# One core, attention into a mixture of experts: when a planner puts eight small transfers on the SP queue

## The chip, the core and the metric

The kernel runs as one program on one core of a Trainium2 chip. Its time is device microseconds of one execution: 771.33 us is the median of three (770.04 to 773.77). The engines work side by side, each through its own list of instructions: PE (matmul), DVE and ACT (elementwise), POOL, and SP, which computes nothing here and issues DMA transfers from one queue; an instruction whose wait isn't over holds those behind it in its list.

## The reference, cut to what matters

Three layers follow one another on 3072 tokens of width 384:

```python
x = attn(q, k, v, alpha)                      # a decaying state per head, scanned over 768 steps
expert_idx = argmax(logits(x), 1)             # 8 experts; gate_w = the winner's softmax share
out[mask] = gate_w[mask, None] * (relu(x[mask] @ w1[e]) @ w2[e])   # per expert e, 384 -> 1024 -> 384
h = out @ w_in                                # 384 -> 2048, float64 weights
return maximum(0.01 * h, h) @ w_out           # 2048 -> 384
```

Every product of weights is done as three float16 products of a high and a low half (hi*hi, hi*lo, lo*hi) that are summed in PSUM.

## The kernel before, in words

**Three stages.** The first (to about 168 us) does the attention and the routing, and scatters each token's row into a DRAM buffer `bucket`, sorted by expert; a row holds the 384 values, a scale, the gate and the token's number. The second (168 to 400 us) runs the experts 0 to 7 one after the other. The third (400 us to the end) is the dense layer, with results scattered by token.

**An expert.** It takes up to 432 rows of `bucket` (`CAP`). `gather` loads them (`xg`), `block` scales and splits them on ACT (L977) and DVE (L978) into four pieces `xs`, and transposes each piece with a DMA from SP's queue (L980) into `xt`. `up` multiplies `xt` by `w1` (L1038 to L1040, eight groups of nine matmuls) and splits the relu on ACT and DVE (L1045, L1046); `down` multiplies by `w2` (L1064 to L1066, three groups of 24) and writes the result into the columns of `x2` that belong to the expert (L1075 on ACT is the high half, L1076 on DVE the low half; the planner calls the latter `("x2l", e, d)`). `xt`, the weight sets and the PSUM tiles are double or fourfold, so the next expert's inputs are made while one runs.

**Weights.** They come as float32 through five staging tiles `wstage` (`fetch`, L989, 384 KB each), and ACT and DVE split them: L994 and L995 for expert weights (eight pieces an expert), L1011 to L1017 for the third stage's float64 weights (`double`, four pieces an expert). A fetch must wait until the staging tile of five fetches earlier has been read.

**Scales and tokens.** `put_meta(e)` (L938 to L944) copies two numbers of each of the expert's 432 rows from `bucket` to a compact DRAM buffer `meta`, at an offset that SP loads from SBUF (L941, for e above 0). The transfers of successive experts overlap in `meta`, so each waits until the one before has landed. `scales` (L948) loads `meta` into `ms` after the last, and a cast on DVE (L949) makes the token numbers `tki`. Both are first used in the third stage.

**Clears.** `clear` zeroes the columns of `x2` above the first expert's, 12 ACT instructions (L1085), before expert 1 writes there.

**The planner.** The order of the second stage's instructions on each engine is computed ahead by `Plan`: a list schedule in which an operation has an engine, a duration, the keys it reads and writes, and `at`. It takes the operation that can start first; `at` decides only among those within 0.15 us of it. An operation that depends on another of the same engine may start when that one has been *issued*, without its landing:

```python
t = max([free.get(eng, 0.0)] + [end[d] + self.HOP if ops[d][0] != eng else start[d] + ops[d][1] for d in deps])
...
first = min(best)[0]
t, _, _, i = min((b for b in best if b[0] <= first + 0.15), key=lambda b: b[1:])
```

The keys named in `after` are dependencies of the plan alone. The waits that the engines obey come from the tiles and buffers that an instruction reads and writes. `begin(e)` is 5.5 + 26.4 e.

Of the kernel before, what the change touches and what calls it, by code (L numbers as in the profile page):

```python
# [34 lines left out]
CAP = 432  # L35
# [140 lines left out]
def body(ctx, tc, qT, kT, aT, v, emb, tau, w1, w2, w_in, w_out, out):  # L176
# [6 lines left out]
    bucket = dram.tile([E * NT, AUG], F32, name="bucket")  # L183
    bviews = dram_disjoint_views(bucket, NC)
    meta = dram.tile([X2, 2], F32, name="meta")
# [62 lines left out]
    class Jobs:  # L248
# [20 lines left out]
        def add(self, jobs):  # L269
            self.todo += jobs  # L270
            self.fetch()
# [11 lines left out]
    with tc.tile_pool(name="at", bufs=1) as rt, \  # L283
# [58 lines left out]
        plan = Plan()  # L342
        NU = B * NP
        V, S_, T_, G_, Q_ = "DVE", "ACT", "PE", "POOL", "SP"
# [556 lines left out]
    with tc.tile_pool(name="mx", bufs=1) as mxp, \  # L901
# [10 lines left out]
        size = [min(P, CAP - n * P) for n in range(NB)]  # L912
        NF = CAP // P
        plan = Plan(rate=230e3, land=4.0)
        V, S_, T_, G_, Q_ = "DVE", "ACT", "PE", "POOL", "SP"
        START, TURN = 5.5, 26.4

        def begin(e):
            return START + TURN * e

        def gather(e):
            xg = xgs[e % 2]

            def block(n):
                nc.sync.dma_start(xg[:size[n], n], bucket[e * NT + n * P:e * NT + n * P + size[n]])

            def most():
                nc.sync.dma_start(xg[:, :NF], bucket[e * NT:e * NT + NF * P].rearrange("(n p) d -> p n d", p=P))
                for n in range(NF, NB):
                    block(n)  # L930

            if e < 2:
                for n in range(0 if e else E0 // P, NB):
                    plan.add(Q_, 0.45, lambda n=n: block(n), ["bucket"], [("xg", e), ("row", e, n)], size=(P * AUG * 4, 2.5), at=float(e))
            else:
                plan.add(Q_, 0.9, most, ["bucket"], [("xg", e % 2)] + [("row", e % 2, n) for n in range(NB)], size=CAP * AUG * 4, at=begin(e - 2) + 8,
                         after=[("xt", 1, NB - 1, 0)] if e == 2 else ())

        def put_meta(e):
            def go():  # L940
                so = nc.sync.value_load(offi[0:1, e:e + 1], min_val=0, max_val=NT) if e else 0  # L941
                nc.sync.dma_start(meta[ds(so, CAP) if e else slice(0, CAP)], bucket[e * NT:e * NT + CAP, D + 1:D + 3])

            plan.add(Q_, 1.5, go, ["bucket"], ["meta"], at=begin(e) + 4, size=(CAP * 64, 5.0))  # L944

        def scales():

# [21 lines left out]
        def block(e, n):  # L969

            m, g = size[n], len(turned) % 4
            turned.append(n)
            x, r = xgs[e % 2][:m, n, :D], xgs[e % 2][:m, n, D:D + 1]
            xs, xt = xs16[g][:m], xts[e % 2]
            at = begin(e - 1) + 1.0 + 4.0 * n if e > 1 else n - 15.0
            got = ("row", e % 2, n)
            plan.add(S_, 0.62, lambda: nc.scalar.activation(xs[:, 0], x, AF.Copy, scale=r), [got], [("xs", g, 0)], at=at)  # L977
            plan.add(V, 0.61, lambda: nc.vector.scalar_tensor_tensor(xs[:, 1], x, r, xs[:, 0], op0=ALU.mult, op1=ALU.subtract),  # L978
                     [got, ("xs", g, 0)], [("xs", g, 1)], at=at)
            plan.add(Q_, 1.25, lambda: nc.sync.dma_start_transpose(out=xt[:, :, n * P:n * P + m], in_=xs.rearrange("p i d -> p (i d)")),  # L980
                     [("xs", g, i) for i in range(2)], [("xt", e % 2, n, i) for i in range(2)], size=(230e3, 5.0), at=at + 1.0)
# [50 lines left out]
        def up(e, f, xt, at, cols, early=False):  # L1032
            (w1h, w1l), n = shaped(sets[e % 2])[:2], cols.stop - cols.start
            ps, hh, hl = ps1[f % 4][:, :n], hid[0][f][:, cols], hid[1][f][:, cols]

            def go():
                for k in range(KD):
                    nc.tensor.matmul(ps, w1h[:, f, k], xt[:, k], start=k == 0, stop=False)  # L1038
                    nc.tensor.matmul(ps, w1h[:, f, k], xt[:, KD + k], start=False, stop=False)  # L1039
                    nc.tensor.matmul(ps, w1l[:, f, k], xt[:, k], start=False, stop=k == KD - 1)  # L1040

            rows = [("sg", i) for i in range(2)] if early else [("xt", e % 2, b, i) for b in range(cols.start // P, NB) for i in range(2)]
            key = ("h", f, early)
            plan.add(T_, 9 * step(n), go, [("w", e % 2, 0, f // 2, i) for i in range(2)] + rows, [("ps1", f % 4)], at=at)
            plan.add(S_, 0.16 + n / 1200, lambda: nc.scalar.activation(hh, ps, AF.Relu), [("ps1", f % 4)], [(*key, 0)], at=at)  # L1045
            plan.add(V, 0.155 + n / 960, lambda: nc.vector.scalar_tensor_tensor(hl, ps, 0.0, hh, op0=ALU.max, op1=ALU.subtract), [("ps1", f % 4), (*key, 0)], [(*key, 1)], at=at)  # L1046
# [3 lines left out]
        def places(e):  # L1050
            def on(eng, n):
                offset[n] = eng.value_load(offi[0:1, e:e + 1], min_val=0, max_val=NT)

            plan.add(S_, 0.1, lambda: on(nc.scalar, 0), [], [("place", 0)], at=begin(e) + 4)
            plan.add(V, 0.1, lambda: on(nc.vector, 1), [], [("place", 1)], at=begin(e) + 4)

        def down(e, d, at, cols, early=False):
            (w2h, w2l), n = shaped(sets[e % 2])[2:], cols.stop - cols.start
            b = (KD * e + d) % 4
            ps, ds_ = ps2[b][:, :n], slice(d * P, (d + 1) * P)  # L1060

            def go(f):
                hh, hl = hid[0][f][:, cols], hid[1][f][:, cols]
                nc.tensor.matmul(ps, w2h[:, f, ds_], hh, start=f == 0, stop=False)  # L1064
                nc.tensor.matmul(ps, w2h[:, f, ds_], hl, start=False, stop=False)  # L1065
                nc.tensor.matmul(ps, w2l[:, f, ds_], hh, start=False, stop=f == NF1 - 1)  # L1066

            for f in range(NF1):
                plan.add(T_, 3 * step(n), lambda f=f: go(f), [("w", e % 2, 1, f // 2, i) for i in range(2)] + [("h", f, early, i) for i in range(2)], [("ps2", b)], at=at + 0.05 * f)

            def place(i):
                return cols if e == 0 else ds(offset[i], CAP)

            where = [[("place", i)] * (e > 0) + [("clear", i, d)] * (e == 1) for i in range(2)]
            plan.add(S_, 0.16 + n / 1200, lambda: nc.scalar.activation(x2[0][d][:, place(0)], ps, AF.Copy, scale=2.0 ** -8), [("ps2", b)] + where[0], [("x2", e, d)], at=at)  # L1075
            plan.add(V, 0.155 + n / 960, lambda: nc.vector.scalar_tensor_tensor(x2[1][d][:, place(1)], ps, 2.0 ** -8, x2[0][d][:, place(1)], op0=ALU.mult, op1=ALU.subtract),  # L1076
                     [("ps2", b), ("x2", e, d)] + where[1], [("x2l", e, d)], at=at)

        def clear(d, at):

            w = (NT - CAP) // 4
            for n in range(2):
                for o in range(CAP, NT, 2 * w):
                    x = x2[n][d][:, o:o + 2 * w].bitcast(F32)
                    plan.add(S_, 0.16 + w / 1200, lambda x=x: nc.scalar.activation(x, row0[:, 0:1].to_broadcast([P, w]), AF.Copy), ["bucket"], [("clear", n, d)], at=at)  # L1085
# [5 lines left out]
        def pieces_of(e):  # L1091
            mine = [(begin(e) + 4.0 + 2.9 * j, weights, e + 1, j) for j in range(2 * KD * F1 // CH if e + 1 < E else 0)]
            mine += [(begin(e) + 5.0 + 5.8 * j, *second[e * per + j]) for j in range(min(per, len(second) - e * per))]
            return sorted(mine, key=lambda x: x[0])
# [16 lines left out]
        for e in range(E):  # L1111
            if e:
                add(pieces_of(e))
            cols = slice(0 if e else E0, CAP)
            for f in range(NF1):
                up(e, f, xts[e % 2][:, :, cols], begin(e) + 1.65 * f - 12.0, cols)
                if e + 1 < E and f < NB:
                    block(e + 1, f)
                if f == 2:
                    put_meta(e)  # L1120
                if f == 4 and e + 2 < E:
                    gather(e + 2)
            if e:
                places(e)
            for d in range(KD):
                down(e, d, begin(e) + 13.2 + 4.4 * d - 12.0, cols)
            if e == 0:
                for d in range(KD):
                    clear(d, begin(1) + 4.0 * d)
        scales()  # L1130
        for i in plan.order():
            plan.ops[i][2]()
# [2 lines left out]
    with tc.tile_pool(name="gp", bufs=1) as gp:  # L1135
# [9 lines left out]
        plan = Plan()  # L1145
# [240 lines left out]
```

## Time and profile before

| | us |
|---|---|
| median of three executions | 771.33 |
| the profiled execution, its own time | 768.53 |
| its span, first to last instruction | 766.8 |
| PE busy | 730.8 (95%) |
| DVE busy | 602.4 (79%) |
| ACT busy | 389.0 (51%) |
| the chain that ended last: PE | 81% of the span |
| the same: DMA `meta<-bucket` | 3% of the span |

A group of the profile names the source line, the engine, the operation and its tiles as out<-in. In the timelines, the first two numbers are start and duration in us, and square brackets hold the idle time ahead of the instruction and what ended it. In the span cut into 40 slices of 19.2 us, PE is at 9 tenths or more in the second and third stages except in slices 8 and 11 to 12 counted from 0, and the slice 230 to 249 us has PE at 4 tenths and its granted clock at 6 tenths.

### The profile page before, as it was taken

How to read it: one execution, taken by the hardware profiler on the slowest of the kernel's cores; microseconds unless marked ns; L12 is line 12 of the kernel's file. 1: busy time of each engine (PE TensorE's matmuls, PEld its weight loads, DVE VectorE, ACT ScalarE, POOL GpSimd, SP SyncE). 2: the span in 40 equal slices, each digit the busy share in tenths (PEclk: the TensorE clock that was granted, in tenths of full speed). 3: DMA queues.
4: the chain of work that ended last, by engine and by line, in shares of the span. 5: the costliest groups of instructions: out<-in, count | busy, mean ns of one | idle time of the engine just before them, and what ended most of it. 6: DMA issues, size and time to landing. Idle time of an engine off the chain costs nothing.

```text
span 766.8 us, 16571 instructions
## 1 busy us (share of the span) xinstructions
PE 730.8 (95%) x6775; PEld 561.6 (73%) x6775; DVE 602.4 (79%) x1131; ACT 389.0 (51%) x746; POOL 87.6 (11%) x91
## 2 busy tenths in 40 slices
PE   7999999989984999999999999999999999999995
PEld 3777766658742555555558777999999999999995
DVE  7989889967727887889879888878778768778771
ACT  2343455537916666777656444544434435535430
POOL 4120715150000000000000010010110110110101
PEclk9999999999996999999999999999999999999999
DMA  8983946247829866878610000000000000000001
GB/s 295 340 272 130 276 151 208 64 146 191 195 34 286 239 201 192 246 212 209 194 60 1 12 12 11 12 23 1 22 22 1 23 22 2 22 12 12 21 11 35
DMA packets 61968, 84.70 MB, mean 110 GB/s; under 512 B 29880, under 2 KB 41152, under 8 KB 61888
## 3 DMA queue, kind: packets, MB, share of 16 engines
q1 hardware_dynamic: 58656, 74.09, 33.8%
q0 software_dynamic: 3072, 9.49, 3.3%
q8 instruction: 55, 0.90, 0.5%
q14 instruction: 25, 0.20, 0.1%
q10 hardware_dynamic: 160, 0.01, 0.0%
HBM read 66.83 MB, written 12.12 MB: 103 GB/s over the span
## 4 chain that ended last, share of the span: by engine, by line
PE 81%; DMA 7%; DVE 7%; ACT 3%; issue 1%; POOL 0%; SPq 0%; POOLq 0%; DVEq 0%; ACTq 0%
PE ps L829 8%; PE ps L828 8%; PE ps L827 8%; PE ps L861 6%; PE ps L863 6%; PE ps L862 6%; PE ps L1038 4%; PE ps L1039 4%; PE ps L1040 4%; PE ps L1066 4%; PE ps L1065 4%; PE ps L1064 4%; DMA meta<-bucket 3%; PE psc L409 2%; PE py L462 2%; DMA wstage<-in_w 2%
## 5 line engine op out<-in xcount | busy, mean ns | idle before, releaser
L827 PE MATMUL ps<-x2h,wih 128*128 128x256 f16 x576 | 157.0, 273 | 0.0
L828 PE MATMUL ps<-x2l,wih 128*128 128x256 f16 x576 | 157.0, 273 | 0.0
L829 PE MATMUL ps<-x2h,wil 128*128 128x256 f16 x576 | 157.0, 273 | 0.0
L835 DVE TENSOR_TENSOR held<-ps,held 128x512 f32<-128x512 f32 x96 | 65.8, 686 | 51.3 <-ACT held L834 51.3
L834 ACT ACTIVATE held<-ps 128x512 f32<-128x512 f32 x96 | 57.2, 596 | 78.1 <-PE ps L829 77.9
L895 POOL DMA_INDIRECT out<-wstage,tki x24 | 25.4, 1060 | 559.2 <-ACT wstage L1202 302.3
L1038 PE MATMUL ps<-xt,w1h 128*128 128x432 f16 (+1 forms) x192 | 64.3, 336 | 15.7 <-DMA xt<-xs 14.8
L1065 PE MATMUL ps<-held,w2h 128*128 128x432 f16 (+2 forms) x216 | 70.2, 326 | 0.5 <-DVE held L1046 0.5
L1066 PE MATMUL ps<-held,w2l 128*128 128x432 f16 (+2 forms) x216 | 70.2, 326 | 0.0
L1064 PE MATMUL ps<-held,w2h 128*128 128x432 f16 (+2 forms) x216 | 70.2, 326 | 0.0
L1039 PE MATMUL ps<-xt,w1h 128*128 128x432 f16 (+1 forms) x192 | 64.3, 336 | 0.5 <-DVE xt L964 0.5
L1040 PE MATMUL ps<-xt,w1l 128*128 128x432 f16 (+1 forms) x192 | 64.3, 336 | 0.0
L827 PEld LDWEIGHTS <-wih 128*128 128x128 f16 x576 | 56.4, 98 | 6.8
L828 PEld LDWEIGHTS <-wih 128*128 128x128 f16 x576 | 56.4, 98 | 6.7
L829 PEld LDWEIGHTS <-wil 128*128 128x128 f16 x576 | 56.4, 98 | 6.5
L1045 ACT ACTIVATE held<-ps 128x432 f16<-128x432 f32 (+2 forms) x72 | 35.2, 489 | 26.6 <-PE ps L1040 22.6
L1046 DVE SCALAR_TENSOR_TENSOR held<-ps,held 128x432 f16<-128x432 f32 (+2 forms) x72 | 39.3, 552 | 11.8 <-ACT held L1045 11.6
L1038 PEld LDWEIGHTS <-w1h 128*128 128x128 f16 x216 | 21.6, 100 | 32.4 <-issue 15.8
L874 DVE SCALAR_TENSOR_TENSOR wstage<-ps,ms,wstage 128x192 f32<-128x192 f32 x80 | 31.9, 411 | 16.6 <-PE ps L863 16.5
L349 PE MATMUL pfill<-busy,ones 128*128 128x512 f16 x122 | 40.0, 400 | 2.0 <-POOL busy L194 2.0
L846 ACT ACTIVATE o1h<-held 128x256 f16<-128x256 f32 (+1 forms) x40 | 20.9, 523 | 30.7 <-DVE held L835 29.9
L846 ACT ACTIVATE o0h<-held 128x256 f16<-128x256 f32 (+1 forms) x40 | 20.9, 523 | 30.3 <-DVE held L835 29.7
(267 smaller groups left out, 1904.8 us busy)
## 6 DMA issues: line engine op xcount, KB each, us to landing
wstage<-in_w SPq DMA_DIRECT2D x64, 384.0 KB, 4.2
a<-in_aT SPq DMA_DIRECT2D x16, 387.5 KB, 5.4
k<-in_kT SPq DMA_DIRECT2D x16, 384.0 KB, 5.9
q<-in_qT SPq DMA_DIRECT2D x16, 384.0 KB, 6.6
wstage<-in_w_in SPq DMA_DIRECT2D x16, 384.0 KB, 4.4
wstage<-in_w_out SPq DMA_DIRECT2D x16, 384.0 KB, 3.4
v<-in_v SPq DMA_DIRECT2D x8, 576.0 KB, 8.8
xg<-bucket SPq DMA_DIRECT2D x6, 582.0 KB, 5.7
```

The lines of the kernel that those rows point to most:

```text
L827: nc.tensor.matmul(d, wih[:, k, fs], xs[0][k], start=k == 0, stop=False)
L828: nc.tensor.matmul(d, wih[:, k, fs], xs[1][k], start=False, stop=False)
L829: nc.tensor.matmul(d, wil[:, k, fs], xs[0][k], start=False, stop=k == KD - 1)
L834: add("ACT", 0.59, lambda: nc.scalar.activation(dst, src, AF.Copy, scale=0.01), [key], [("g", i)])
L835: add("DVE", 0.69, lambda: nc.vector.tensor_tensor(dst, src, dst, op=ALU.max), [key, ("g", i)], [("g", i)])
L861: nc.tensor.matmul(d, oh, wh, start=k == 0, stop=False)
L1038: nc.tensor.matmul(ps, w1h[:, f, k], xt[:, k], start=k == 0, stop=False)
L1039: nc.tensor.matmul(ps, w1h[:, f, k], xt[:, KD + k], start=False, stop=False)
L1040: nc.tensor.matmul(ps, w1l[:, f, k], xt[:, k], start=False, stop=k == KD - 1)
L1064: nc.tensor.matmul(ps, w2h[:, f, ds_], hh, start=f == 0, stop=False)
L1065: nc.tensor.matmul(ps, w2h[:, f, ds_], hl, start=False, stop=False)
L1066: nc.tensor.matmul(ps, w2l[:, f, ds_], hh, start=False, stop=f == NF1 - 1)
```

## The change

Two arguments to the planner. `put_meta(e)` for e above 0 gets an `after` on `("x2l", e - 1, 0)`, the low half of the first third of the preceding expert's result, and is entered with 0.9 us instead of 1.5. The clears get an earlier `at`. What the instructions do stays; only their order on the engines can differ.

```diff
-            plan.add(Q_, 1.5, go, ["bucket"], ["meta"], at=begin(e) + 4, size=(CAP * 64, 5.0))
+            plan.add(Q_, 0.9, go, ["bucket"], ["meta"], at=begin(e) + 4, size=(CAP * 64, 5.0), after=[("x2l", e - 1, 0)] if e else ())
...
-                    clear(d, begin(1) + 4.0 * d)
+                    clear(d, begin(0) + 8.0 + 4.0 * d)
```

## Rows read from the trace of the kernel before

**Rows 1.** Timeline of PE: start, duration, instruction, in brackets idle and releaser.

```profile
199.95 0.35 PE L1038 MATMUL ps<-xt,w1h 128*128 128x432 f16 x1
...
226.05 0.35 PE L1066 MATMUL ps<-held,w2l 128*128 128x432 f16 x1
241.18 0.52 PE L1038 MATMUL ps<-xt,w1h 128*128 128x432 f16 x1 [14.78 <-DMA xt<-xs]
...
244.37 0.43 PE L1038 MATMUL ps<-xt,w1h 128*128 128x432 f16 x1
...
387.35 0.35 PE L1064 MATMUL ps<-held,w2h 128*128 128x432 f16 x1
```

**Rows 2.** Busy time of stretches: length; PE, PEld, DVE, ACT, POOL; PE clock, DMA share, GB/s.

```profile
190.00:200.00 10.00, 9.50 (x126) 9.35 (x124) 8.69 (x20) 10.00 (x23) 0.00 (x0) 1.00 0.83 207
...
219.00:222.50 3.50, 3.50 (x21) 1.89 (x20) 0.00 (x0) 0.00 (x0) 0.00 (x0) 1.00 0.07 1
...
241.20:244.40 3.20, 3.20 (x10) 1.32 (x11) 2.87 (x7) 2.13 (x5) 0.00 (x0) 0.50 1.11 341
...
295.70:321.90 26.20, 26.20 (x146) 14.06 (x144) 23.86 (x42) 20.42 (x39) 0.00 (x0) 1.00 0.79 221
```

**Rows 3.** Chain that ended last, 197 to 246 us: start, duration, what.

```profile
200.22 6.36 DMA meta<-bucket
...
221.91 3.82 DMA meta<-bucket
...
225.74 0.40 SPq L948
...
226.25 4.97 DMA wstage<-in_w
...
234.17 6.92 DMA xt<-xs
```

**Rows 4.** Timeline of SP's queue in the second stage, merged where a line repeats.

```profile
188.18 7.18 SPq L980 DMA_TRANSPOSE xt<-xs  x4
...
211.19 11.26 SPq L942 DMA_DIRECT2D meta<-bucket  x4
...
227.95 2.62 SPq L980 DMA_TRANSPOSE xt<-xs  x2
...
372.31 1.23 SPq L989 DMA_DIRECT2D wstage<-in_w  x2
```

**Rows 5.** Timeline of DVE in the second stage.

```profile
203.32 0.56 DVE L1013 SCALAR_TENSOR_TENSOR t<-wstage,t 128x384 uint32<-128x384 uint32 x1
...
215.89 0.60 DVE L978 SCALAR_TENSOR_TENSOR xs<-xg,xs 48x384 f16<-48x384 f32 x1
232.53 0.56 DVE L1017 SCALAR_TENSOR_TENSOR wil<-t,wih 128x384 f16<-128x384 f32 x1 [16.03 <-ACT wih L1016]
...
367.86 0.61 DVE L1076 SCALAR_TENSOR_TENSOR x2l<-ps,x2h 128x432 f32 x1 [1.40 <-ACT x2h L1075]
...
385.96 0.95 DVE L995 SCALAR_TENSOR_TENSOR w2l<-wstage,w2h 128x768 f16<-128x768 f32 x1
```

**Rows 6.** All instructions of a tile, durations min/median/max in ns; then landing in us.

```profile
L980 SPq DMA_TRANSPOSE xt<-xs x28: 1187/1223/2904, 188.2 to 345.9; - x28
...
DMA to landing us min/median/max: 2.5/4.2/6.9
```

**Rows 7.** Timeline of ACT: the first and the last of the 12 clears, and a later weight.

```profile
181.95 0.74 ACT L1085 ACTIVATE x2h<-row 128x660 f32<-128x660 f32 x1
...
205.98 0.74 ACT L1085 ACTIVATE x2l<-row 128x660 f32<-128x660 f32 x1
...
378.29 0.84 ACT L994 ACTIVATE w2h<-wstage 128x768 f16<-128x768 f32 x1
```

**Rows 8.** First use of `ms`, by source line: durations in ns, first and last start.

```profile
L1202 ACT ACTIVATE wstage<-ps,ms x4: 580/580/581, 436.0 to 481.0; 128x384 f32<-128x384 f32 x4
```

## The prediction

> **What bounds the kernel now.** I read the page's 40 slices first: the one place after the attention where PE falls far below full is the slice 230 to 249 us, and its clock falls there too. The timeline of PE shows why: the last matmul of expert 1 starts at 226.05, the first of expert 2 at 241.18, held by the DMA that transposes its tokens [rows 1]. Everywhere else from 244 us to the end of the expert stage PE is full: the turn of expert 4, 26.2 us long, has 26.20 busy at clock 1.00 [rows 2]. The chain of waits then tells what made the transposes late. From 200.22 it goes through six `meta<-bucket` landings one after the other to the `ms` load at 225.74, a weight fetch at 226.25, and the transpose at 234.17 that lands at 241.09 [rows 3]. SP's queue issues four of these metas in a row from 211.19, and nothing else between [rows 4]. Each of these transfers of 864 numbers stops the queue for 3.8 to 6.4 us [rows 3], because the next must wait for its landing. In 219.0 to 222.5 neither DVE nor ACT does anything, and the DMA engines are at 0.07 [rows 2]: the feed is starved, not slow.
>
> The cause is readable in the planner. It lets an SP operation start when the SP operation it depends on was issued, so the chain of metas looks to it like 1.5 us fillers for any idle moment of SP. It had idle moments, and put all eight ahead of expert 2: the `ms` load, which follows the last, was issued at 225.74 [rows 3].
>
> **What the change removes.** The six `meta` landings and the `ms` load leave the stretch 200 to 226. With `after` on a DVE result, each meta can be planned only once the preceding expert's first third is out, so metas 1 to 7 come about one turn apart, and each finds its predecessor long landed: no wait on SP. PE then passes from expert 1 to 2 as early as the inputs allow.
> - Cadence: 199.95 to 226.05 is 143 steps, 0.1825 us each, so expert 1 would hand over at 226.23 [rows 1]. The gap is 241.18 - 226.23 = 14.95 us.
> - Clock: nine matmuls from 241.18 to 244.37 take 3.19 us where nine steps are 1.64 [rows 1]; the clock was granted at 0.50 (1.2 GHz) in that stretch, after the idle, and at 1.00 in a turn without idle [rows 2]. That is 1.55 us more, which goes with the idle time.
> - Together 16.5 us, the ceiling of this part.
>
> **What is late next.** Expert 2's first group needs all four transposed pieces. Their last DVE half was done at 215.89 + 0.60 = 216.5 [rows 5]. A staging tile for the weight fetch that went out at 226.25 was free after 203.32 + 0.56 = 203.9 [rows 5], so that fetch and the transposes queued behind it [rows 4] can go some 20 us earlier. From 216.5, a transpose lands 2.5 to 6.9 us later, median 4.2 [rows 6], so at 219.0 to 223.4: before 226.23. But with SP unblocked, more weight pieces reach DVE earlier and may be ordered ahead of that last half: two at 0.95 us [rows 5] and their companions on ACT at 0.84 [rows 7], up to 4 us. That gives 219 to 227.4, an idle time of 0 to 1.2 us; with a second delay of the same size for a full DMA system (the share was 1.11 in 241.2 to 244.4 [rows 2]) 0 to 5. By the median it is 216.5 + 1.9 + 4.2 = 222.6, so I take 0 and keep 5 as the end.
>
> DVE lost 16.03 us to the same stall [rows 5], so the feed moves forward by about as much as PE does and their distance later on stays. This matters, as a turn has 23.86 us of DVE work in 26.2 [rows 2]: there is no room to catch up much.
>
> **What the moved metas cost.** Issue time is the same as before. On the DMA engines one meta alone took 0.07 of 3.5 us [rows 2], 0.25 us of all sixteen; seven beside the weights are 1.7 us in seven turns that leave about a fifth of the DMA time free (0.79 in use [rows 2]). Nothing, then; at worst a whole landing of 6.4 us [rows 3] is added once to a fetch behind it.
>
> The last one is different. `ms` must still wait for meta 7 to land, and it now does so near the end of expert 6, just after an x2l like that at 367.86 [rows 5], with `w2` of expert 7 behind it on SP. The planner still ignores that wait. SP would be held for 3.8 to 6.4 us [rows 3]; of the fetches behind it, those issued from 372.31 wait 0 to 3 us, and the first of these is converted at 378.29 [rows 7], some 6 us after its issue, where a fetch took 4.97 to land [rows 3]. The cast of the token numbers can hold DVE some 3 us for the same reason. The last piece of `w2` for expert 7 is ready at 386.91 [rows 5]; PE needs it near 390.6: the down part starts at 387.35 [rows 1], and 18 steps of 0.1825 precede the quarter that reads it. So 3.7 us of cover: cost 0 to 3, I take 0. The use of `ms` at 436.0 [rows 8] stays some 60 us away.
>
> The Trainium skill prices such a wait lower: in "DMA: Bandwidth & Descriptors", section "Anatomy of one DMA", the fixed part of a transfer is put at about 2.0 us, fitted on transfers that GpSimd issues. By that figure, an estimate, SP would be held 2 us at meta 7, the cost above would be 0 at both ends, and the sum the same without its upper bound. The rows show 3.8 to 6.4 us for the same transfer here, and the measurement decides.
>
> **What the clears do.** 12 instructions of 0.74 us [rows 7], 8.9 us, the same work. `at` decides only ties, and ACT was full in 190 to 200 [rows 2], so there it does decide: conversions of expert 1's `w2` and of later pieces move back by up to 8.9 us. They are needed at 199.95 + 13.1 = 213 and later. The pieces of expert 1's tokens have an earlier `at` and can only be held by one clear each; their four transposes end on SP at 195.36 [rows 4] and land about 198 to 199.9, close to PE's 199.95. Bounds: four holds of 0.74 in a row, 3.0 us lost, or 0.5 won where PE was at 9.50 of 10 [rows 2]. I take 0, as a single hold about fits between landing and use.
>
> **Sum.** 768.53 (span 766.8 and 1.73 around it) - 16.5 = 752.0 for the profiled execution. For small waits of the kind bounded above, each taken as 0 though none can be below it, I add 0.7: 752.7. The median of three stood 2.8 above the profiled execution, so 755.5 against 771.33, a gain of 15.8.
>
> **Rivals.**
> - *Part of the wait stays.* Expert 2's transposes are held by weight pieces that now go first, PE idles 3 to 5 us and starts at the lower clock again (1.6): 755.5 + 5 to 7, near 761. For it: the DVE order can change and a transpose can need 6.9 us. Against: 9.7 us between 216.5 and 226.23.
> - *`ms` behind meta 7 costs the end of the stage.* SP held up to 6.4 us and DVE 3 us against 3.7 us of cover, 2 to 3 us of PE: 758. For it: 23.86 of 26.2 on DVE. Against: fetches are issued some 6 us before use.
> - *The stall only changes its name.* If the queue's next wait is for staging tiles and the transposes stand behind those, PE idles nearly as long: 767.5 to 772. Against: a tile was free at 203.9, and DVE and ACT were idle for want of data.
> - *Slower: the tie becomes a true wait.* If SP really waited at each meta for x2l, the place is seven turns, with weights of the next expert behind. The cover is 3.7 us at the weights and about 1 at the fetch; beyond a hold of 4.7 us each further us is PE idle time, with 1.6 for the clock if the idle is long. At a hold of 7 us, seven turns cost 7 x (2.3 + 1.6) = 27 us, against 16.5 won: 782 on the scale of the median. It decides from a hold of about 5.5 us. Against: the meta touches only `bucket`, `meta` and an offset, and `after` is read by the planner alone.
>
> **Chances.** Forecast 0.68 (its own range 752.5 to 758), part of the wait stays 0.13, the end of the stage 0.10, changed name 0.05, slower 0.04. The measurement can tell about 0.5%, 3.9 us. So faster 0.91, same 0.05, slower 0.04. The range 752 to 763 takes in the first three and leaves out the last two and an edge of the first.
>
> **What would show it.** Right: no `meta` in the chain between 200 and 241; metas of SP about 26 us apart, each without a wait; PE's idle time before expert 2 gone or under 3 us; the granted clock 1.00 through 226 to 245; the `ms` load after 340 us, held 3 to 6 us by meta 7. Wrong: PE idle on `xt`, `w1` or `w2` in any expert for more than 5 us in sum, or a wait of a meta for DVE.

## The result, and the profile after

| | before | after |
|---|---|---|
| median of four executions | 771.05 us (770.04 to 773.77) | 748.34 us (748.05 to 749.60) |
| profiled execution | 768.53 | 748.28 |
| its span | 766.8 | 746.6 |
| PE busy | 730.8 (95%) | 727.2 (97%) |

The ratio is 0.9703, with a 95% interval of 0.9676 to 0.9730: faster by 22.7 us. Which chips these executions ran on isn't known; compared on one chip, below, the gain was 20.7 and 20.0 us. The forecast of 755.5 had the direction and the mechanism, but the time fell 7.2 us below it and 3.7 us below the low end of its range.

The stall of [rows 1] is gone. Timeline of PE after (start, duration, instruction, in brackets the idle time and its releaser): the first matmul of the second stage, the first of expert 1, the last and first around the start of expert 2, the first of the third stage.

```profile
167.69 0.27 PE L1038 MATMUL ps<-shared,w1h 128*128 128x256 f16 x1 [0.41 <-DVE ohs L761]
...
196.28 0.35 PE L1038 MATMUL ps<-xt,w1h 128*128 128x432 f16 x1
...
222.38 0.35 PE L1066 MATMUL ps<-held,w2l 128*128 128x432 f16 x1
222.56 0.35 PE L1038 MATMUL ps<-xt,w1h 128*128 128x432 f16 x1
...
380.24 0.27 PE L827 MATMUL ps<-x2h,wih 128*128 128x256 f16 x1
```

Expert 2 follows expert 1 by one step, 0.18 us. From 196.28 to 380.24 there are 183.96 us, seven turns of 26.28 us. Everything that PE waits for between 167 and 384 us is in this list of its waits after (engine, line, what it waits for: us in total, times, longest):

```profile
PE pkv L757 <- DVE c L755: 1.4, 1, 1.4
PE ps L1039 <- DVE xt L964: 0.5, 1, 0.5
PE ps L1038 <- ACT xt L963: 0.4, 1, 0.4
PE ps L1038 <- DVE ohs L761: 0.4, 1, 0.4
```

All four lie ahead of expert 1. Two windows after (columns as in [rows 2]) have the clock at 1.00 and PE full, also in 220 to 230 us, where before DVE and ACT stood idle [rows 2, 5]:

```profile
170.00:180.00 10.00, 10.00 (x94) 8.96 (x92) 6.28 (x14) 6.15 (x15) 2.41 (x3) 1.00 0.53 162
...
220.00:230.00 10.00, 10.00 (x56) 5.37 (x55) 8.80 (x17) 6.30 (x13) 0.00 (x0) 1.00 1.10 282
```

What made the room is in the timeline of SP's queue. The metas, four in a row before [rows 4], stand about a turn apart, and the `ms` load follows the last one:

```profile
180.29 0.66 SPq L942 DMA_DIRECT2D meta<-bucket  x1
...
197.60 0.61 SPq L942 DMA_DIRECT2D meta<-bucket  x1
...
215.87 0.63 SPq L942 DMA_DIRECT2D meta<-bucket  x1
...
242.54 0.60 SPq L942 DMA_DIRECT2D meta<-bucket  x1
...
347.60 0.57 SPq L942 DMA_DIRECT2D meta<-bucket  x1
352.16 0.41 SPq L948 DMA_DIRECT2D ms<-meta  x1
```

In SP's waits after, one row of this kind is left, the hold of the `ms` load; no meta waits:

```profile
SPq L948 <- DMA meta<-bucket: 4.0, 1, 4.0
```

In those of before, from 167 to 404 us, there were two:

```profile
SPq L942 <- DMA meta<-bucket: 12.9, 5, 3.6
...
SPq L948 <- DMA meta<-bucket: 3.2, 1, 3.2
```

The chain that ended last after, by engine, has 1% of DMA and no meta among its lines, where before the meta alone had 3%:

```profile
PE 89%; DVE 6%; ACT 2%; DMA 1%; issue 1%; POOL 1%; POOLq 0%; ACTq 0%; DVEq 0%
```

**Where the 20.2 us of span went** (766.8 to 746.6), from the starts of the same matmuls in the two timelines. The shared part is expert 0's first 256 columns, whose input lies in the tile `shared`; its other 176 columns come from `xt`.

| part | before | after | difference |
|---|---|---|---|
| expert 1 to third stage | 200.54 | 183.96 | 16.58 |
| `up` of the shared part, in before partly at half clock | 9.53 | 7.86 | 1.67 |
| from there to expert 1 | 21.83 | 20.73 | 1.10 |
| start of the second stage | 168.59 | 167.69 | 0.90 |
| third stage | 366.31 | 366.36 | -0.05 |

The first row is the stall with its clock. The second was not seen ahead of the result: in the profiled execution of before, a stretch of the shared part ran at the lower clock with no wait in it. The two waits ahead of it, 1.44 and 0.41 us, the second at 168.59, stand the same in after, which has no such stretch. Timeline of PE before, the edges of the stretch:

```profile
169.25 0.27 PE L1038 MATMUL ps<-shared,w1h 128*128 128x256 f16 x1
169.36 0.33 PE L1039 MATMUL ps<-shared,w1h 128*128 128x256 f16 x1
169.48 0.42 PE L1040 MATMUL ps<-shared,w1l 128*128 128x256 f16 x1
...
172.88 0.27 PE L1038 MATMUL ps<-shared,w1h 128*128 128x256 f16 x1
```

In 170 to 180 us the clock before was granted at 0.86 on average, against 1.00 after in the window above. The third row is the clears. They gave 1.10 us: the pieces that ACT makes for expert 0 come sooner, and the `held` of its last groups is no longer waited for. Timeline of PE before, two waits:

```profile
187.73 0.24 PE L1038 MATMUL ps<-xt,w1h 128*128 128x176 f16 x1 [0.95 <-ACT xt L963]
...
196.39 0.24 PE L1065 MATMUL ps<-held,w2h 128*128 128x176 f16 x1 [0.50 <-DVE held L1046]
```

And after, where the first is shorter and the second is gone:

```profile
184.66 0.24 PE L1038 MATMUL ps<-xt,w1h 128*128 128x176 f16 x1 [0.44 <-ACT xt L963]
```

The fourth lies ahead of the second stage: before, a weight fetch at 86.35 us stood on the chain with a landing of 10.16 us, and PE waited 0.46 and 0.45 us behind it (at 98.19 and 99.49); after has neither wait.

### The profile page after: what moved, and what is told of

The parts are those of the page before. It is cut to its first block, busy times and chain, and to the rows that moved or that the text cites. A ratio compares the mean times of both kernels' runs of the same rounds, so it can differ in the third digit from the quotient of the medians.

```text
span 746.6 us, 16582 instructions
## 1 busy us (share of the span) xinstructions
PE 727.2 (97%) x6775; PEld 560.0 (75%) x6775; DVE 601.5 (81%) x1131; ACT 388.6 (52%) x746; POOL 87.0 (12%) x91
## 4 chain that ended last, share of the span: by engine, by line
PE 89%; DVE 6%; ACT 2%; DMA 1%; issue 1%; POOL 1%; POOLq 0%; ACTq 0%; DVEq 0%
PE ps L828 8%; PE ps L827 8%; PE ps L829 8%; PE ps L863 6%; PE ps L862 6%; PE ps L861 6%; PE ps L1039 4%; PE ps L1040 4%; PE ps L1064 4%; PE ps L1066 4%; PE ps L1065 4%; PE ps L1038 4%; PE psc L409 3%; PE py L428 3%; PE py L462 2%; PE pfill L349 2%
## 5 line engine op out<-in xcount | busy, mean ns | idle before, releaser
L1045 ACT ACTIVATE held<-ps 128x432 f16<-128x432 f32 (+2 forms) x72 | 34.6, 485 | 20.7 <-PE ps L1040 20.4
L386 POOL TENSOR_TENSOR rc<-q,bc 128x768 f32<-128x768 f32 x15 | 25.9, 1726 | 84.8 <-DVE kh L384 70.0
```

## The experiments

The theory: the planner lets an SP operation start once the SP operation it depends on is issued, not landed; so the metas pile up ahead of expert 2, each holds SP for a landing, and the tie only spreads them. Rivals: the clears give a part of it; the shorter cost (0.9 for 1.5) does it; the seven spread metas still cost; what exceeded the forecast is the chip or the execution. Four runs shared one chip, the next four a second, the last four a third. "Before" beside a time is the kernel before on the same chip. A ratio with its 95% interval comes from all the executions and need not be the quotient of the two medians.

**The kernel before, again.** No edit.

> The kernel before, unchanged, to see how much of the missed 7 us is spread between its own executions. Theory: the order did what was forecast, 16.5 us of expert 2's wait, and the rest is where this kernel's executions differ from one another (the clock after the routing, the length of the six landings). Then the ratio is 1.00 within 0.002, the spread of the executions is 3 us or more (770 to 774), and the second profile shows a different number in at least one of: the matmuls at half clock after 168 us (17 of 0.42 us in the first profile), the idle time before expert 2 (14.78). Rival: all executions of this order are alike and the change gained 22 us by itself; then the second profile repeats the first within 0.5 us at each of these places and in the sum.

774.68 us, before 771.88, ratio 1.0013 (0.9990 to 1.0036): the same kernel twice on one chip, with medians 2.8 us apart, its twelve executions here between 771.03 and 777.25. The stall is there (13.37 us on `xt`; expert 1 to third stage 199.09 us). But this profile loses time in the attention, too. Its timeline of ACT, and then of PE:

```profile
160.60 0.71 ACT L473 ACTIVATE yT<-py 112x384 f32<-112x384 f32 x2 [5.18 <-remote]
```

```profile
161.14 0.82 PE L490 MATMUL ptr<-ident,yT 112*128 112x112 f32 x3 [3.52 <-ACT yT L473]
```

ACT stood 5.18 us for a releaser that the profile calls only "remote" (in before 1.93 us, for PE), and PE 3.52 with it; the clock was then granted at 0.53 in 160 to 170 us, and the second stage began at 175.63 instead of 168.59. It is in all eight profiles of the first and third of these chips, whichever kernel ran, and in none of the other six: four of the second chip, and the two of before and after shown above. So absolute times are compared on one chip only.

**The tie alone.** The new line of `put_meta`, clears as before.

```diff
-            plan.add(Q_, 1.5, go, ["bucket"], ["meta"], at=begin(e) + 4, size=(CAP * 64, 5.0))
+            plan.add(Q_, 0.9, go, ["bucket"], ["meta"], at=begin(e) + 4, size=(CAP * 64, 5.0), after=[("x2l", e - 1, 0)] if e else ())
```

> The change's tie and the 0.9 us alone, with the clears' earlier `at` taken back. Theory: the tie carries the 16.5 us and more or less all of the rest; the clears move at most 1.1 us (expert 0's last part was 0.4 and 0.7 us shorter after the change). 748.5 to 750, 0.970 to 0.973 of before, and no PE wait above 1 us after 190 us. Rival: the clears carry some 5 us of the surplus: 753 to 755.

757.38 us, ratio 0.9793 (0.9761 to 0.9824). The 748.5 to 750 expected was missed, with the hold in the attention in this profile too. Expert 1 to third stage takes 183.96 us, as after: the tie, entered with the shorter cost, takes the whole stall.

**The clears alone.**

```diff
-                    clear(d, begin(1) + 4.0 * d)
+                    clear(d, begin(0) + 8.0 + 4.0 * d)
```

> The clears' earlier `at` alone, metas as before. Theory: the metas still hold SP, so PE still waits 13 to 18 us before expert 2: 769 to 772, ratio 0.997 to 1.002. Rival (the clears carry the surplus): 764 to 766, with the gain ahead of 200 us.

773.29 us, ratio 1.0001 (0.9977 to 1.0026): nothing. The metas still hold SP, at other places (six waits of 13.9 us in all), and PE's one long wait has become five of 0.75 us and more, three of them here in its timeline:

```profile
221.23 0.34 PE L1038 MATMUL ps<-xt,w1h 128*128 128x432 f16 x1 [4.08 <-DVE held L1046]
...
233.24 0.52 PE L1064 MATMUL ps<-held,w2h 128*128 128x432 f16 x1 [2.38 <-ACT held L1045]
...
247.48 0.36 PE L1038 MATMUL ps<-xt,w1h 128*128 128x432 f16 x1 [1.71 <-DMA xt<-xs]
```

Expert 1 to third stage is 199.68 us. What the clears give early, the stall takes back.

**The planner counts every landing, no tie.**

```diff
-... end[d] + self.HOP if ops[d][0] != eng else start[d] + ops[d][1] for d in deps])
+... end[d] + self.HOP if ops[d][0] != eng or self.lands and ops[d][8] else start[d] + ops[d][1] for d in deps])
...
-        plan = Plan(rate=230e3, land=4.0)
+        plan = Plan(rate=230e3, land=4.0, lands=True)
```

> The kernel before with one edit in the planner of the expert stage instead of the change: an operation that depends on a transfer of its own engine waits for the planned landing. Metas keep their 1.5 us and have no tie. Theory: what cost the time is that the planner took the chain of metas for fillers without landings; with the landing counted it spaces them some 6.7 us apart, SP is hardly held, and the wait before expert 2 goes: 747 to 752. Rival: it is the distance of a whole turn that matters, because each landing in reality varies (3.4 to 6.4 us) and an early cluster still holds the transposes: 757 to 768, with a wait of 5 us or more before expert 1 or 2.

764.84 us, ratio 0.9889 (0.9860 to 0.9919): 7.0 us, about half of the 14.5 of the tie alone on that chip, and not the 747 to 752 us expected. The long stall is gone, but the rule also moved other transfers, and in its timeline PE waits where it had not:

```profile
193.03 0.38 PE L958 MATMUL ps<-ident,xs 48*128 48x48 f32 x3 [2.53 <-DVE xs L960]
...
210.50 0.34 PE L1038 MATMUL ps<-xt,w1h 128*128 128x432 f16 x1 [1.88 <-DMA xt<-xs]
...
238.76 0.36 PE L1038 MATMUL ps<-xt,w1h 128*128 128x432 f16 x1 [1.82 <-DMA xt<-xs]
```

From the second stage's start to expert 1 it takes 37.87 us, the tie alone on the same chip 31.29. From expert 1 to the third stage it takes 185.95 us. This neither proves nor refutes the cause: the rule moved too much else, hence the narrower one below.

**The changed kernel, on the second chip.** No edit.

> The changed kernel, unchanged, beside executions of the kernel before on the same chip. So far the second profile of the kernel before (and three variants of it) shows one thing that its first profile and that of the changed kernel do not: near 155 us ACT is held some 3 us longer ahead of a copy of yT (L473, 5.2 us instead of 1.9, releaser unknown), PE then idles 3.5 us and its clock is halved for most of the routing, 5 to 7 us in sum. Theory A: that hold belongs to the chip or the hour; then the changed kernel shows it too here, 753 to 757, and the forecast of 755.5 would have been right there. Theory B: it belongs to the program as laid out; the changed kernel is free of it: 747 to 750, PE's idle ahead of the yT transposes under 1 us.

748.14 us, before 768.82 (15 executions, 766.43 to 771.33), ratio 0.9730 (0.9708 to 0.9751): 20.7 us. The time after repeats to 0.2 us; the time before is 2.2 below the 771.05 measured first, and within 0.3 of the execution profiled then.

**The tie alone, on the second chip.** As above.

> The tie without the clears once more, beside the changed kernel on the same chip. Theory A (chip or hour): it differs from the changed kernel by 1 to 3 us, which is what expert 0's part shows (0.5 + 0.7, and 1.6 where the clock is halved). Theory B (program): 755 to 759 again, 8 to 10 us over the changed kernel, of which 5 lie ahead of 168 us.

750.16 us, ratio 0.9749 (0.9724 to 0.9773). Beside the changed kernel's 748.14 the clears are worth 2.0 us. From the second stage's start to expert 1 the rows have 29.69 us here and 28.59 after, 1.10, the same as in the table above. Another 0.58 is an earlier start of the second stage (168.01 against 167.43 in the changed kernel's profile on this chip), ahead of all clears; so I take 1.1 as theirs, and 2.0 as the most. The two waits of expert 0 are back in this profile, 0.95 and 0.50 us, as in before.

**The shorter cost, no tie.**

```diff
-            plan.add(Q_, 1.5, go, ["bucket"], ["meta"], at=begin(e) + 4, size=(CAP * 64, 5.0))
+            plan.add(Q_, 0.9, go, ["bucket"], ["meta"], at=begin(e) + 4, size=(CAP * 64, 5.0))
```

> The kernel before with 0.9 us instead of 1.5 for a meta, no tie and the clears as before. Theory: metas stay a chain at the start and are packed closer, one landing after another on SP; the wait moves ahead to expert 1 or stays at expert 2, 10 to 18 us of PE idle time: 766 to 776. Rival: the shorter entry is what spreads them: under 760.

769.81 us, ratio 1.0006 (0.9992 to 1.0021): nothing. SP waits 17.7 us in six metas, and PE's timeline has the stall in three pieces, the first ahead of expert 1:

```profile
204.63 0.52 PE L1038 MATMUL ps<-xt,w1h 128*128 128x432 f16 x1 [5.92 <-DMA xt<-xs]
...
225.17 0.34 PE L1064 MATMUL ps<-held,w2h 128*128 128x432 f16 x1 [2.09 <-ACT held L1045]
...
232.42 0.52 PE L1065 MATMUL ps<-held,w2h 128*128 128x432 f16 x1 [6.91 <-DVE held L1046]
```

**Metas 1 to 7 left out.** Clears as before, and only expert 0's meta is transferred.

```diff
-                if f == 2:
+                if f == 2 and e == 0:
```

> The kernel before with the transfers of experts 1 to 7 left out (their scales and tokens are then not in meta, and ms follows meta 0 at once). No tie, clears as before. What the metas cost where they are now is read against this. Theory: the tie hides them all, so this is not faster than the tie alone by more than 1 us: 747 to 758, whichever stage 1 has, and from expert 1 to the third stage within 0.5 us of 183.96. Rival: the seven spread metas still cost something beside the weights: 2 us or more faster from expert 1 to the third stage.

751.73 us, ratio 0.9763 (0.9736 to 0.9789). Expert 1 to third stage is 183.96 us again, so seven spread metas cost PE nothing. The median is 1.6 us above the tie alone; in the profiled executions, 2.2 us apart, 1.67 is a half-clock stretch in the shared part like that of before (9.53 us against 7.86) and 0.53 a later start of the second stage.

**The planner counts the landing of the metas alone, no tie.**

```diff
-... end[d] + self.HOP if ops[d][0] != eng else start[d] + ops[d][1] for d in deps])
+... end[d] + self.HOP if ops[d][0] != eng or d in self.lands else start[d] + ops[d][1] for d in deps])
...
+            plan.lands.add(len(plan.ops) - 1)
```

> The kernel before, where the planner of the expert stage counts the planned landing for the chain of metas alone (the earlier variant counted it for all of SP's transfers, and by that also spread the first loads of xg, which held expert 0 and 1 by 6 us). No tie, clears as before. Theory: the missing landing is the cause. Metas come 7 us or more apart in the plan, SP is held by none for more than 2 us, no PE wait of over 1 us after 190 us, 183.96 us from expert 1 to the third stage: like the tie alone, 749 to 751.5 (756 to 759 where ACT is held near 155 us). Rival: metas must be a turn apart; real landings beside the weights (4.3 to 7.5 us) still add up, 5 us or more before expert 2.

755.27 us, before 774.56, ratio 0.9764 (0.9740 to 0.9787); the changed kernel beside it 754.58. Its metas on SP, by line (durations in ns, first and last start), end in the turn of expert 3, and none waits:

```profile
L942 SPq DMA_DIRECT2D meta<-bucket x8: 545/597/672, 184.7 to 275.3; - x8
```

Expert 1 to third stage: 183.98 us. So the cause is the landing that the planner doesn't count: without a tie, and with the old 1.5 us, counting it for the metas alone removes the stall. The tie is one cure, the true cost in the planner another.

**Four metas in a row, later.** The changed kernel, with metas 4 to 7 tied to expert 3's result.

```diff
-... after=[("x2l", e - 1, 0)] if e else ())
+... after=[("x2l", min(e - 1, 3), 0)] if e else ())
```

> The changed kernel, but metas 4 to 7 are all tied to expert 3's result, so four of them and the load of ms stand in a row on SP near 270 us, in the middle of the stage. It prices a hold of SP where the feed is in step. Theory: SP is held some 4 x 4 to 6 = 16 to 24 us, of which the stage's buffers and the early fetches cover 6 to 10; PE waits 8 to 15 us on w1, w2 or xt of expert 4 or 5 and starts at the lower clock (1.6): 757 to 765. Rival: the wait before expert 2 needed the cluster early in the stage, where nothing had been fetched ahead; in the middle it is covered: 748 to 751.

763.39 us, ratio 0.9847 (0.9826 to 0.9869), 8.8 us above the changed kernel on that chip. Timeline of SP, then of PE, then a window:

```profile
279.46 14.06 SPq L942 DMA_DIRECT2D meta<-bucket  x4
...
297.28 0.39 SPq L948 DMA_DIRECT2D ms<-meta  x1
```

```profile
300.29 0.54 PE L1064 MATMUL ps<-held,w2h 128*128 128x432 f16 x1 [3.32 <-ACT w2h L994]
```

```profile
300.00:303.60 3.60, 3.22 (x9) 1.17 (x10) 1.48 (x3) 1.15 (x4) 0.00 (x0) 0.50 0.84 235
```

The stall is back, smaller than the 8 to 15 us expected, and its name is now `w2`. Expert 1 to third stage is 192.86 us, 8.9 more: idle time of 3.9 us in three waits, and nearly all of the rest the clock, at half from 300.3 to about 309.8.

**The clears first of all.** The changed kernel, with the clears before all other work of ACT.

```diff
-                    clear(d, begin(0) + 8.0 + 4.0 * d)
+                    clear(d, d - 45.0)
```

> The changed kernel with the clears entered before everything else of the stage (`at` from -45). Theory: what the clears gave was that ACT's clears stopped falling between expert 0's last results; put ahead of all they cost expert 0's own splits, PE waits for held or xt in 170 to 190: 0.5 to 3 us slower than the changed kernel beside it. Rival: the earlier the better, up to 1 us faster than the changed kernel (then it would beat both).

759.47 us, ratio 0.9807 (0.9792 to 0.9822), 4.9 above the changed kernel on that chip, where 0.5 to 3 was expected. The twelve clears stand together on ACT (183.12 to 190.92), the pieces for expert 0 behind them, and in PE's timeline:

```profile
192.33 0.30 PE L1038 MATMUL ps<-xt,w1h 128*128 128x176 f16 x1 [3.51 <-ACT xt L963]
```

Behind this wait the clock was granted at 0.50 from 193.1 to 198.3 us. Expert 1 to third stage is 183.95 us, so the loss lies ahead of it. The place of the clears is worth something in both directions.

**The changed kernel, on the third chip.** No edit.

> The changed kernel beside the variant with the clears first, for the comparison on one chip: 748 to 750, as on two chips so far (756 or so where ACT is held near 155 us). From expert 1 to the third stage 183.96 within 0.1.

754.58 us, ratio 0.9745 (0.9725 to 0.9766): 20.0 us. Its profile has the hold in the attention too (second stage from 175.63), and 183.96 us from expert 1 to the third stage.

## Why the forecast was right, and where it failed

- *What the change removes*: right. Forecast 16.5 us, measured 16.58; and the tie alone has the same 183.96 us from expert 1 to the third stage. One reading under it was wrong: 3.8 to 6.4 us are the landings on the chain (the shortest of the six was 3.4), not the time that SP stood. Between the first two of these metas SP issued two weight fetches, at 201.29 and 201.75. By its own waits it stood 16.1 us in all, for five metas and the `ms` load, 3.6 us at most. The 16.5 did not hang on this, as it was read from PE's rows.
- *What is late next*: right in the value taken, 0. No wait remains from expert 1 on. The bound of 5 us was not touched.
- *What the moved metas cost*: 0, shown by leaving them out. The hold of SP at meta 7 was 4.0 us, inside 3.8 to 6.4, and cost PE nothing. The Trainium skill's "DMA: Bandwidth & Descriptors" says in "Two DMAs through the same engine are not ordered" that the issuing engine should wait for the first transfer's completion even where both are on one queue. The trace has such waits, 12.9 us of them before; what happens without them no run here shows. The 2.0 us that the Trainium skill gives for the fixed part (same page, "Anatomy of one DMA"), fitted on transfers that GpSimd issues, is below what SP's metas took here: landings after were 4.3 to 7.5 us, and the hold 4.0.
- *What the clears do*: taken as 0, with a bound of 0.5 us won; both were too low. They gave 1.1 us in the rows, and at most 2.0 in times. The lines that showed it were at hand, 0.95 and 0.50 us of waits in expert 0; the working looked only at what the clears might hold after their move, not at what they had held before it.
- *Sum*: this step failed. It carried the profiled execution over to the kernel after, and put an offset and an allowance on top. Of the miss of 7.2 us, 2.7 is the offset, which did not carry over (2.8 for three executions before, 0.06 after, and 0.3 for fifteen executions of before on the second chip); 0.7 is the allowance for small waits, of which none came; 1.1 is the clears; 0.1 the stall; and 2.5 (1.67 + 0.90, less 0.05 in the third stage) was time of that one execution which the execution after did not have. Together 7.1. Even without the offset the sum would have been 752.7, still 4.4 too high.

The offset could have been questioned from the start: three executions had 771.33, 770.04 and 773.77, none as low as the profiled 768.53. Later, on the second chip, the median of fifteen was 768.82. The highest of the three lies above all fifteen of the second chip (766.43 to 771.33) and inside those of the first (770.16 to 776.75) and third (770.75 to 775.66), where ACT is held. So part of the offset, and of the 22.7 us, may be the chip; this stays open.

On the second chip the mean granted clocks mostly go with the times. Of the fifteen, eight lie at 768.19 to 768.85 with 0.987 (a ninth of that clock has 770.34), and the two slowest, 771.15 and 771.33, have 0.983. After, in the nine executions of two measurements, those at 0.998 lie at 748.01 to 748.28, and the four at 0.995 or 0.996 from 748.39 to 749.88. The kernel before varies there by some 5 us, the one after by under 2. That this part goes with the stall is not shown, and two runs speak against it: the shorter cost without a tie keeps a stall, and its ten executions vary by 2.4 us with no order by clock; the changed kernel on the third chip, with ACT held in the attention, has no stall and varies by 3.7. Timed executions have no timeline.

The rivals: a part of the wait did not stay; the end of the stage cost nothing; the stall kept no other name; and the tie became no true wait (no meta waits for DVE). That the stall can change its name, the runs with the clears alone and with the shorter cost do show: there, and not here, the gain was lost to it.

Open stays why `up` of the shared part has a half-clock stretch in three of the fourteen profiles (before, metas left out, every landing counted) and not in the others. Late clears alone don't bring it: the kernel before again, the tie alone (twice), the shorter cost and the landing of the metas alone have clears as late and no such stretch.

## What to carry to other kernels

A planner that counts a dependent transfer's issue but not its landing will use it as a filler in an in-order queue; look for the same small transfer several times in a row on a queue, each held by the one before, and count the landing for that chain alone: a rule for all transfers lost about half of the gain here. Where work is moved, price what it held at its old place as well as what it will hold at the new one. Don't carry an offset between a profiled execution and a median of three over to another kernel's sum: here it was 2.8 us, as much as two medians of one kernel on one chip differed, and 0.3 with more executions on another chip.

## What the runs showed of the hardware

- A hold of ACT of 5.0 to 5.2 us, ending at 160.2 to 161.6 us, whose releaser the profile calls only "remote", in all eight profiles of two chips and in none of the six others, where the same instruction waited 1.93 us for PE. The second stage began 3 to 8 us later (171.7 to 175.6 against 167.4 to 168.6). In the eight, the clock in 162 to 170 us was granted at 0.50 (four of them) or at 0.74 to 0.86. The kernels before and after both have it on those chips: the gain was 20.7 us without it and 20.0 with it.
- A wait of 3.3 us on PE was followed by 9.5 us at half clock, with two more waits of 0.3 us in them (the four metas in a row); one of 14.78 us by some 3 us [rows 1, 2]. The price of a stall in clock does not grow with its length in these two.
